# Four feature blocks per step for one-tile chunks in a fused attention and two-layer kernel

## The chip, the cores and the metric

The kernel runs on one core of a Trainium2 chip. The metric is the device time of one execution in microseconds. Three runs of the kernel before gave 1259.59, 1261.18 and 1263.39 us, median 1261.18.

## The reference

The inputs are q, k and v of shape (4 batches, 8 heads, 576 positions, 64), and five weights. Attention keeps, in each row of scores, the 32 largest and softmaxes over them. Its output, as 2304 tokens of 512 features, goes through two layers:

```python
scores = scale * np.matmul(q, k.transpose(0, 1, 3, 2))
kth = np.partition(scores, -32, axis=-1)[..., -32:-31]
scores = np.where(scores >= kth, scores, -1e9)
attn = softmax(scores)                  # rows of 576
x = np.matmul(attn, v)                  # -> 2304 x 512
gate = 1.0 / (1.0 + np.exp(-(x @ w_gate)))        # 512 -> 1536
x = (gate * (x @ w_val)) @ w_out                  # 1536 -> 512
g = np.maximum(x @ w_in, 0.0) ** 2                # 512 -> 2048
out = g @ w_out2                                  # 2048 -> 512, float32
```

## The kernel before

The 2304 tokens are 18 tiles of 128. They are worked in 12 chunks (line 29): chunks 0 to 5 hold one tile each, chunks 6 to 11 two. For every chunk, attention is done first (8 heads per tile: scores on TensorE, four rounds of the eight largest on VectorE, the exponential on ScalarE, the transposed weights times the values on TensorE), then the two layers.

N is the number of tokens in a chunk, 128 or 256. Chunks 0 and 1 use a function of their own in float32 (`moe32`, lines 902 to 996). Chunks 2 to 11 split every operand into a high and a low float16 part and use three products of these per block (`SPLIT`, line 694). A feature block is 128 features: the first layer has NF1 = 12 of them, the second NF2 = 16.

One step of layer 1 is `l1_pair` (lines 744 to 770). For two feature blocks it makes the gate matmuls into a bank `pg` and the value matmuls into a bank `pv` (12 matmuls of N columns for each block), then a chain: Tanh on ScalarE (line 763), an add-and-multiply on GpSimd (764), the product with `pv` on VectorE (765), the high part as a cast on ScalarE (768), the low part as a difference on GpSimd (769). `l1_acc` (lines 780 to 800) then multiplies the result by `w_out` into two accumulators. It is written one step behind `l1_pair`, so that a step's chain runs beside the next step's matmuls.

Between the layers the accumulators are squared and summed for a scale (lines 822 to 830) and split in two parts (832, 833). One step of layer 2 is `l2_pair` (851 to 872): matmuls into a bank `ph`, ReLU (867) and Square (869) on ScalarE, a square in float32 and a difference on GpSimd (870, 871); then `l2_acc` (874 to 885) with the output weights, written DEPTH2 = 3 steps behind. After the last step the output is copied (897) and stored.

The tiles `pg`, `pv` and `ph` share two PSUM banks (pool `ps_w`, 512 float32 columns each); the accumulators have two, attention four. The activation tiles `th`, `gh`, `r`, `rh` and the output tile share four buffers of the tag `hi` (HIB, line 27). From chunk 4 on (`PRE0`, line 41), a chunk calls `start` for the first two steps of the next chunk near its own end of layer 1 (lines 811, 836); their results have a buffer of their own, `gp`.

The order of the work on each engine is not written out. The kernel is written as a list of instructions with priorities, and a planner runs a simulated time at build and puts each engine's instructions in order by priority and by when they can start, giving out buffers as they come free. Each engine then takes its instructions strictly in that order. Attention is written into this list by `attend` (line 1162): after each step of a chunk's layers, as many units of attention (one head of one tile) are written, with a higher priority, as `step` asks (line 1253), so that a whole chunk's attention is spread evenly over the steps of the chunk before.

Of the kernel before, what the change touches and what calls it, by code (L numbers as in the profile page):

```python
# [8 lines left out]
F16 = mybir.dt.float16  # L9
BF16 = mybir.dt.bfloat16  # L10
F32 = mybir.dt.float32
# [3 lines left out]
AF = mybir.ActivationFunctionType  # L15
ALU = mybir.AluOpType
# [5 lines left out]
P = 128  # L22
# [3 lines left out]
M4 = 3  # L26
HIB = 4
DEPTH2 = 3
CHUNKS = [[0], [1], [2], [3], [4], [5]] + [[i, i + 1] for i in range(6, 18, 2)]
AHEAD = 1000  # L30
LEAD = 10
# [8 lines left out]
NPRE = 2  # L40
# [29 lines left out]
TB = 15  # L70
# [3 lines left out]
def tile_topk_attention__then__two_moe_layers(  # L74
# [11 lines left out]
    chunks=None,  # L86
    upto=None,
):
    nc = tc.nc
    B, H, S, D = q.shape  # L90
# [3 lines left out]
    KM = DM // P  # L94
    NF1 = F1 // P
    NF2 = F2 // P
# [8 lines left out]
    if chunks is None:  # L105
        chunks = CHUNKS

# [3 lines left out]
    mpool = ctx.enter_context(tc.tile_pool(name="mpool", bufs=1))  # L111
# [172 lines left out]
    class Pair:  # L284


        def __init__(self, ci, hp, xt):
            self.ci, self.hp, self.xt = ci, hp, xt
            self.tts = chunks[ci]
            self.N = len(self.tts) * P  # L290
            self.segs = segments(ci)
# [234 lines left out]
        def values(self):  # L526
            xp = ps_t.tile([P, 512], F32, tag="tr", name=f"xp_{self.ci}_{self.hp}")
            for si, (b, o, n) in enumerate(self.segs):
                for c in range(NB):
                    for j in range(2):  # L530
# [12 lines left out]
                        )  # L543
            nc.scalar.copy(self.xt[:, self.hp, :], xp[:, 0 : self.N])

# [143 lines left out]
    def wblk(name, a, kt, f0, n):  # L689
        t, e = parts[(name, kt, f0 // 512)]  # L690
        return t[:, a, e, f0 % 512 : f0 % 512 + n]

    xsl = {}
    SPLIT = ((0, 0), (0, 1), (1, 0))
# [26 lines left out]
    class Moe:  # L721
        pass

    ahead = {}

    def start(ci):

        m = ahead[ci]
        if m.gp is None:
            m.gp = mpool.tile([P, NPRE, 2, 2 * m.N], F16, tag="m4", bufs=M4, name=f"gp_{ci}")  # L730
        fp = len(m.queue)
        m.queue.append((fp, m.l1_pair(fp, m.gp[:, fp])))

    def moe_head(ci, x):
        m = ahead[ci] = Moe()
        m.gp, m.queue = None, []
        tts = chunks[ci]
        N = len(tts) * P
        ig = scales["wg"][1]
        xs, ix = x  # L740
        gsc = xsmall[ci].bitcast(F32)[:, 4:5]
        nc.vector.scalar_tensor_tensor(gsc, ix, 0.5, ig, op0=ALU.mult, op1=ALU.mult)

        def l1_pair(fp, gh=None):
            pg = ps_w.tile([P, 512], F32, tag="wk", name=f"pg_{ci}_{fp}")
            pv = ps_w.tile([P, 512], F32, tag="wk", name=f"pv_{ci}_{fp}")
            for pp, wd in ((pg, "wg"), (pv, "wv")):
                for e in range(2):
                    f0 = (2 * fp + e) * P
                    n = 0  # L750
                    for c in range(KM):
                        for a, b_ in SPLIT:
                            nc.tensor.matmul(  # L753
                                pp[:, e * N : (e + 1) * N],
                                wblk(wd, a, c, f0, P),
                                xs[:, b_, c, :],
                                start=(e == 0 and n == 0),
                                stop=(n == 3 * KM - 1),
                                skip_group_check=True,
                            )  # L760
                            n += 1
            th = mpool.tile([P, 2 * N], F32, tag="hi", bufs=HIB, name=f"th_{ci}_{fp}")
            nc.scalar.activation(th, pg[:, 0 : 2 * N], AF.Tanh, scale=gsc)  # L763
            nc.gpsimd.tensor_scalar(th, th, 1.0, float(2.0 ** (-TB - 1)), op0=ALU.add, op1=ALU.mult)
            nc.vector.tensor_tensor(th, pv[:, 0 : 2 * N], th, op=ALU.mult)  # L765
            if gh is None:
                gh = mpool.tile([P, 2, 2 * N], F16, tag="hi", bufs=HIB, name=f"gh_{ci}_{fp}")
            nc.scalar.copy(gh[:, 0], th)  # L768
            nc.gpsimd.tensor_tensor(gh[:, 1], th, gh[:, 0], op=ALU.subtract)
            return gh  # L770

        m.N, m.ix, m.l1_pair = N, ix, l1_pair

    def moe(ci, nxt=None):

        m = ahead.pop(ci)
        tts, N, ix, l1_pair = chunks[ci], m.N, m.ix, m.l1_pair
        accs = []

        def l1_acc(fp, gh):  # L780
            if not accs:
                for h in range(2):
                    accs.append(ps_a.tile([P, 512], F32, tag="acc", name=f"acc1_{ci}_{h}"))

            last = fp == NF1 // 2 - 1
            for e, d in sorted(
                ((e, d) for e in range(2) for d in range(KM)),
                key=lambda t: (t[1], t[0]) if last else t,
            ):
                f = 2 * fp + e  # L790
                if True:
                    for x, (a, b_) in enumerate(SPLIT):
                        nc.tensor.matmul(  # L793
                            accs[d // 2][:, (d % 2) * N : (d % 2 + 1) * N],
                            wblk("wo", a, f, d * P, P),
                            gh[:, b_, e * N : (e + 1) * N],
                            start=(f == 0 and x == 0 and d % 2 == 0),
                            stop=(f == NF1 - 1 and x == 2),
                            skip_group_check=True,
                        )  # L800

        queue = m.queue
        depth = max(1, len(queue))
        for fp in range(len(queue), NF1 // 2):
            queue.append((fp, l1_pair(fp)))
            yield
            if len(queue) > depth:
                l1_acc(*queue.pop(0))
# [41 lines left out]

        def l2_pair(fp):
            ph = ps_w.tile([P, 512], F32, tag="wk", name=f"ph_{ci}_{fp}")
            for e in range(2):
                f0 = (2 * fp + e) * P

                terms = [(c, a, 0) for c in range(KM) for a in range(2)] + [(c, 0, 1) for c in range(KM)]
                for n, (c, a, b_) in enumerate(terms):
                    nc.tensor.matmul(  # L858
                        ph[:, e * N : (e + 1) * N],
                        wblk("wi", a, c, f0, P),  # L860
                        x2[:, b_, c, :],
                        start=(e == 0 and n == 0),
                        stop=(n == 3 * KM - 1),
                        skip_group_check=True,
                    )
            r = mpool.tile([P, 2 * N], F32, tag="hi", bufs=HIB, name=f"r_{ci}_{fp}")
            nc.scalar.activation(r, ph[:, 0 : 2 * N], AF.Relu, scale=float(2.0 ** (7 - 2 * TB)))
            gh = mpool.tile([P, 2, 2 * N], F16, tag="hi", bufs=HIB, name=f"rh_{ci}_{fp}")
            nc.scalar.activation(gh[:, 0], r, AF.Square)  # L869
            nc.gpsimd.tensor_tensor(r, r, r, op=ALU.mult)  # L870
            nc.gpsimd.tensor_tensor(gh[:, 1], r, gh[:, 0], op=ALU.subtract)  # L871
            return gh

        def l2_acc(fp, gh):
            for e in range(2):
                f = 2 * fp + e
                for i in range(len(tts)):
                    for x, (a, b_) in enumerate(SPLIT):
                        nc.tensor.matmul(  # L879
                            acc2[i][:, 0:DM],  # L880
                            gh[:, b_, e * N + i * P : e * N + (i + 1) * P],
                            wblk("w2", a, f, 0, DM),
                            start=(f == 0 and x == 0),
                            stop=(f == NF2 - 1 and x == 2),
                        )

        prev = []
        for fp in range(NF2 // 2):
            prev.append((fp, l2_pair(fp)))
            if len(prev) > DEPTH2:  # L890
                l2_acc(*prev.pop(0))
            yield
        for p in prev:
# [108 lines left out]
    nchunk = len(chunks)  # L1002
# [164 lines left out]
    first = [0]  # L1167
    for c in chunks:
        first.append(first[-1] + H * len(c))
    per_chunk = NF1 // 2 + NF2 // 2  # L1170

    base = 100000

    def at(t):
# [63 lines left out]
    for ci in range(len(PLAIN), nchunk):  # L1238
        while ci not in xsp and ci not in ahead:
            attend(emitted[0] + 1, AHEAD)  # L1240
        if ci not in ahead:
            moe_head(ci, xsp.pop(ci))
        nxt = None
        if PRE0 <= ci < nchunk - 1:

            def nxt(c=ci + 1):
                if c not in ahead:
                    while c not in xsp:
                        attend(emitted[0] + 1, AHEAD)
                    moe_head(c, xsp.pop(c))  # L1250
                start(c)

        step = H * len(chunks[min(ci + 1, nchunk - 1)]) / per_chunk
        lead = LEAD if ci < PRE0 else LEAD2
        for n, _ in enumerate(moe(ci, nxt)):
            attend(first[ci + 1] + lead + int((n + 1) * step), AHEAD)
# [33 lines left out]
```

## Time and profile before

| | |
|---|---|
| runs | 1259.59, 1261.18, 1263.39 us |
| span of the profiled execution | 1261.3 us (no time besides the span is shown for it) |
| TensorE busy | 1176.1 us, 93% |
| VectorE busy | 954.8 us, 76% |
| ScalarE busy | 828.6 us, 66% |
| GpSimd busy | 846.5 us, 67% |
| mean clock of TensorE, share of full | 0.978 |
| layers of chunks 2 to 5 | about 316 to 600 us |

The busy time of an engine is the time covered by its instructions; matmuls are pipelined and their ends are modelled. A wait is idle time of an engine ahead of an instruction, put down to the operation that released it last. In a matmul row, "128*128 128x256" means weights of 128 by 128 and 256 moving columns.

### The profile page before, as it was taken

To read this page: it belongs to the slowest core of one execution; us is meant where nothing else is said; L and a number is where in the kernel's file an instruction comes from. 1 tells how busy PE (TensorE), PEld (TensorE's weight loads), DVE (VectorE), ACT (ScalarE), POOL (GpSimd) and SP (SyncE) were. 2 spreads that over 40 slices of the span, in tenths; PEclk is the share of its full clock that TensorE was granted. 3 is DMA by queue.
4 is the path that set the end of the run, shared out by engine and by line. 5 is a ranking of instruction groups with operands and counts; after the bars stand their busy time and mean duration, and the time that the engine had idled before them with its cause. 6 is when DMAs were issued, how large, how long until landed. Compare 5 with 4: busy or idle time off the path is not lost.

```text
span 1261.3 us, 30690 instructions
## 1 busy us (share of the span) xinstructions
PE 1176.1 (93%) x11477; PEld 957.5 (76%) x11477; DVE 954.8 (76%) x1965; ACT 828.6 (66%) x1719; POOL 846.5 (67%) x1294
## 2 busy tenths in 40 slices
PE   6757989999889998899998999999999999999998
PEld 5536877987777877779787778877876887787775
DVE  6998789899977978899988899999789969110010
ACT  4998996577767676677776777776567657322122
POOL 1788774488876577797876987797678659425223
PEclk9986999999989999999999999999999999999999
DMA  7988762223344356665776575567434523200000
GB/s 188 366 298 275 260 199 81 59 76 90 113 131 130 81 125 159 143 136 130 137 157 133 125 181 115 127 140 158 77 73 97 116 54 60 53 2 1 17 1 18
DMA packets 243190, 153.94 MB, mean 122 GB/s; under 512 B 193120, under 2 KB 209504, under 8 KB 243040
## 3 DMA queue, kind: packets, MB, share of 16 engines
q1 hardware_dynamic: 243040, 151.97, 47.7%
q8 instruction: 91, 1.49, 0.5%
q14 instruction: 59, 0.48, 0.1%
HBM read 105.51 MB, written 18.09 MB: 98 GB/s over the span
## 4 chain that ended last, share of the span: by engine, by line
PE 67%; ACT 9%; POOL 7%; DVE 7%; DMA 5%; issue 3%; SPq 2%; POOLq 0%; ACTq 0%; DVEq 0%
PE ph L858 12%; PE acc L879 12%; PE acc L793 8%; PE pg L753 8%; PE pv L753 8%; PE sp L376 5%; PE xp L509 3%; DMA PT<-S 3%; DVE mx L392 2%; PE xp L536 2%; DVE W L399 2%; PE pg L912 1%; PE qpt L336 1%; PE ph L959 1%; PE acc L976 1%
## 5 line engine op out<-in xcount | busy, mean ns | idle before, releaser
L392 DVE MAX8 mx<-W 128x8 f32<-128x576 f32 x432 | 327.9, 759 | 11.2
L399 DVE MATCH_REPLACE8 W<-mx,W 128x576 f32<-128x576 f32 x288 | 213.8, 742 | 0.0
L858 PE MATMUL ph<-x,wi_w 128*128 128x256 f16 (+1 forms) x1920 | 190.9, 253 | 2.7 <-ACT x L832 2.6
L879 PE MATMUL acc<-w_w,rh 128*128 128x512 f16 x768 | 182.2, 379 | 0.9 <-POOL rh L871 0.9
L858 PEld LDWEIGHTS <-wi_w 128*128 128x128 f16 x1920 | 156.4, 99 | 29.0 <-issue 4.0
L753 PE MATMUL pg<-xs,wg_w 128*128 128x256 f16 (+1 forms) x1440 | 148.4, 254 | 1.1 <-ACT th L763 0.8
L753 PE MATMUL pv<-xs,wv_w 128*128 128x256 f16 (+1 forms) x1440 | 143.8, 252 | 5.1 <-DVE th L765 3.7
L376 PE MATMUL sp<-kst,qt 128*128 128x288 f32 x608 | 132.9, 330 | 6.5 <-ACT rh L869 2.5
L457 POOL TENSOR_TENSOR S<-W,S 128x512 f16<-128x512 f32 x192 | 137.0, 735 | 2.1
L379 ACT COPY S<-sp 128x576 f32<-128x576 f32 x144 | 91.8, 638 | 66.3 <-PE sp L376 39.7
L793 PEld LDWEIGHTS <-wo_w 128*128 128x128 f16 x1440 | 119.6, 99 | 19.2 <-issue 7.4
L411 ACT ACTIVATE W<-S,mx 128x576 f32<-128x576 f32 x144 | 111.8, 776 | 30.9 <-DVE mx L392 30.5
L753 PEld LDWEIGHTS <-wg_w 128*128 128x128 f16 x1440 | 118.9, 99 | 17.2 <-issue 1.4
L753 PEld LDWEIGHTS <-wv_w 128*128 128x128 f16 x1440 | 117.4, 98 | 18.1 <-issue 5.8
L765 DVE TENSOR_TENSOR th<-pv,th 128x512 f32<-128x512 f32 (+1 forms) x60 | 34.7, 579 | 125.4 <-PE pv L753 121.0
L879 PEld LDWEIGHTS <-rh 128*128 128x128 f16 x768 | 72.0, 98 | 73.3 <-POOL rh L871 1.2
L392 DVE MAX8 mx<-S 128x8 f32<-128x576 f32 x144 | 107.3, 745 | 25.9 <-ACT S L379 24.1
L793 PE MATMUL acc<-gh,wo_w 128*128 128x256 f16 (+1 forms) x1104 | 105.6, 250 | 4.7 <-ACT gh L768 2.6
L399 DVE MATCH_REPLACE8 W<-mx,S 128x576 f32<-128x576 f32 x144 | 106.9, 742 | 0.0
L455 POOL TENSOR_SCALAR W<-W,bs 128x576 f32<-128x576 f32 x96 | 71.6, 746 | 52.6 <-ACT S L454 47.8
L870 POOL TENSOR_TENSOR r<-r 128x512 f32<-128x512 f32 (+1 forms) x80 | 69.6, 869 | 54.8 <-ACT rh L869 54.1
L376 PEld LDWEIGHTS sp<-kst,qt 128*128 128x128 f32 x608 | 90.8, 192 | 17.5 <-issue 3.8
(246 smaller groups left out, 2331.5 us busy)
## 6 DMA issues: line engine op xcount, KB each, us to landing
kst<-ks SPq DMA_DIRECT2D x112, 288.0 KB, 3.1
v<-vd SPq DMA_DIRECT2D x32, 320.0 KB, 3.3
qn<-in_q_dram SPq DMA_DIRECT2D x128, 64.0 KB, 2.3
wi_r<-in_moe_w_in_dram SPq DMA_DIRECT2D x16, 512.0 KB, 6.2
w_r<-in_moe_w_out_dram SPq DMA_DIRECT2D x16, 512.0 KB, 4.5
v<-in_v_dram SPq DMA_DIRECT2D x56, 128.0 KB, 2.4
wg_r<-in_moe_w_gate_dram SPq DMA_DIRECT2D x12, 512.0 KB, 6.0
wv_r<-in_moe_w_val_dram SPq DMA_DIRECT2D x12, 512.0 KB, 7.3
```

The costliest lines, as they stand in the source:

```text
L376: nc.tensor.matmul(sp[:, e, 0:HALF], l, r, start=(x == 0), stop=(x == len(ops) - 1))
L379: nc.scalar.copy(ss.rearrange("p (e s) -> p e s", e=2), sp[:, :, 0:HALF])
L392: m8 = nc.vector.max(mx[:, min(r, 1)], cur)
L399: nc.vector.match_replace(wk, mx[:, min(r, 1)], cur, NEG)
L411: nc.scalar.activation(wk, ss, AF.Prelu, bias=kth, scale=-1.0, alpha=1.0 / BIG)
L455: nc.gpsimd.tensor_scalar(wk, wk, rz, 1.0, op0=ALU.mult, op1=ALU.mult)
L457: nc.gpsimd.tensor_tensor(pp[:, o : o + e - f], wk[:, f:e], pp[:, f:e], op=ALU.subtract)
L753: nc.tensor.matmul(pp[:, e * N : (e + 1) * N], wblk(wd, a, c, f0, P), xs[:, b_, c, :], start=(e == 0 and n == 0), stop=(n == 3 * KM - 1), ...
L793: nc.tensor.matmul(accs[d // 2][:, (d % 2) * N : (d % 2 + 1) * N], wblk("wo", a, f, d * P, P), gh[:, b_, e * N : (e + 1) * N], start=(f == ...
L858: nc.tensor.matmul(ph[:, e * N : (e + 1) * N], wblk("wi", a, c, f0, P), x2[:, b_, c, :], start=(e == 0 and n == 0), stop=(n == 3 * KM - 1) ...
L870: nc.gpsimd.tensor_tensor(r, r, r, op=ALU.mult)
L879: nc.tensor.matmul(acc2[i][:, 0:DM], gh[:, b_, e * N + i * P : e * N + (i + 1) * P], wblk("w2", a, f, 0, DM), start=(f == 0 and x == 0), s ...
```

## The change

A chunk of N tokens takes W = 512 / N feature blocks per step: four for chunks 2 to 5, two, as before, for chunks 6 to 11. A step's tiles `pg`, `pv`, `ph`, `th`, `gh`, `r`, `rh` are then 512 columns wide for every chunk. Layer 1 of a one-tile chunk has 3 steps in place of 6, layer 2 has 4 in place of 8. In layer 2 the accumulation of a one-tile chunk is written DEPTH1 = 2 steps behind. `start` makes two steps ahead, so eight feature blocks in place of four when the next chunk is chunk 5. The units of attention are spread over 7 steps in place of 14.

```diff
+DEPTH1 = 2
...
+    def per_step(N):
+
+        return 512 // N
+
...
-            m.gp = mpool.tile([P, NPRE, 2, 2 * m.N], F16, tag="m4", bufs=M4, name=f"gp_{ci}")
+            m.gp = mpool.tile([P, NPRE, 2, m.W * m.N], F16, tag="m4", bufs=M4, name=f"gp_{ci}")
...
         N = len(tts) * P
+        W = per_step(N)
...
-                for e in range(2):
-                    f0 = (2 * fp + e) * P
+                for e in range(W):
+                    f0 = (W * fp + e) * P
...
-            th = mpool.tile([P, 2 * N], F32, tag="hi", bufs=HIB, name=f"th_{ci}_{fp}")
-            nc.scalar.activation(th, pg[:, 0 : 2 * N], AF.Tanh, scale=gsc)
+            th = mpool.tile([P, W * N], F32, tag="hi", bufs=HIB, name=f"th_{ci}_{fp}")
+            nc.scalar.activation(th, pg[:, 0 : W * N], AF.Tanh, scale=gsc)
...
-            last = fp == NF1 // 2 - 1
+            last = fp == NF1 // W - 1
             for e, d in sorted(
-                ((e, d) for e in range(2) for d in range(KM)),
+                ((e, d) for e in range(W) for d in range(KM)),
                 key=lambda t: (t[1], t[0]) if last else t,
             ):
...
-        for fp in range(len(queue), NF1 // 2):
+        for fp in range(len(queue), NF1 // W):
...
-            for e in range(2):
-                f0 = (2 * fp + e) * P
+            for e in range(W):
+                f0 = (W * fp + e) * P
...
-            r = mpool.tile([P, 2 * N], F32, tag="hi", bufs=HIB, name=f"r_{ci}_{fp}")
+            r = mpool.tile([P, W * N], F32, tag="hi", bufs=HIB, name=f"r_{ci}_{fp}")
...
-        for fp in range(NF2 // 2):
+        for fp in range(NF2 // W):
             prev.append((fp, l2_pair(fp)))
-            if len(prev) > DEPTH2:
+            if len(prev) > (DEPTH2 if W == 2 else DEPTH1):
                 l2_acc(*prev.pop(0))
...
-        step = H * len(chunks[min(ci + 1, nchunk - 1)]) / per_chunk
+        W = per_step(len(chunks[ci]) * P)
+        step = H * len(chunks[min(ci + 1, nchunk - 1)]) / (NF1 // W + NF2 // W)
```

## Rows read from the trace of the kernel before

**Rows 1.** Stretches: length, busy us of PE, PEld, DVE, ACT, POOL, clock, DMA.

```profile
...
316.00:600.00 284.00, 259.60 (x3496) 224.81 (x3494) 244.34 (x547) 202.21 (x480) 207.89 (x376) 0.97 0.52 128
600.00:1100.00 500.00, 495.06 (x4826) 391.15 (x4825) 427.05 (x886) 338.68 (x710) 378.92 (x622) 1.00 0.54 113
...
```

**Rows 2.** TensorE's waits, 316 to 600 us: waiter, releaser, us, times, longest.

```profile
...
PE kpt L164 <- DMA kn<-in_k_dram: 5.5, 3, 2.8
PE pv L753 <- DVE th L765: 3.7, 1, 3.7
PE acc L793 <- ACT gh L768: 2.6, 1, 2.6
PE sp L376 <- ACT rh L869: 2.5, 1, 2.5
PE acc L793 <- POOL gh L769: 2.0, 2, 1.6
PE acc L793 <- ACT ob L897: 1.9, 1, 1.9
...
PE acc L879 <- POOL rh L871: 0.9, 2, 0.6
PE pg L753 <- ACT th L763: 0.8, 1, 0.8
...
```

**Rows 3.** Timeline, chunk 2's layer 1: start, us, engine, line, operation, [idle before].

```profile
...
333.90 1.50 PE L793 MATMUL acc<-gh,wo_w 128*128 128x128 f16 x24
...
337.17 2.23 DVE L666 SCALAR_TENSOR_TENSOR w_w<-w_c,wsmall,w_w 128x1024 f16<-128x1024 f32 x1
...
339.99 0.40 DVE L765 TENSOR_TENSOR th<-pv,th 128x256 f32<-128x256 f32 x1
...
340.45 2.06 PE L753 MATMUL pv<-xs,wv_w 128*128 128x128 f16 x24 [3.70 <-DVE th L765]
...
342.58 2.46 PE L753 MATMUL pg<-xs,wg_w 128*128 128x128 f16 x24
...
```

**Rows 4.** Timeline of TensorE, end of layer 1 and layer 2 of chunk 2.

```profile
...
357.64 1.50 PE L793 MATMUL acc<-gh,wo_w 128*128 128x128 f16 x24
361.76 0.37 PE L793 MATMUL acc<-gh,wo_w 128*128 128x128 f16 x2 [2.61 <-ACT gh L768]
363.68 2.29 PE L793 MATMUL acc<-gh,wo_w 128*128 128x128 f16 x20 [1.55 <-POOL gh L769]
...
378.68 1.46 PE L879 MATMUL acc<-w_w,rh 128*128 128x512 f16 x6
...
```

**Rows 5.** Timeline, start of layer 2 of chunk 4.

```profile
...
524.49 2.85 PE L858 MATMUL ph<-x,wi_w 128*128 128x128 f16 x48
...
527.76 0.64 ACT L379 COPY S<-sp 128x576 f32<-128x576 f32 x1 [2.37 <-DMA PT<-S]
...
529.84 0.77 PE L376 MATMUL sp<-kst,qt 128*128 128x288 f32 x4 [2.50 <-ACT rh L869]
...
```

**Rows 6.** Instructions on two tiles: count, duration ns min/median/max, first, last, forms.

```profile
...
L764 POOL TENSOR_SCALAR th<-th x60: 395/617/626, 322.0 to 1201.7; 128x512 f32<-128x512 f32 x36, 128x256 f32<-128x256 f32 x24
L765 DVE TENSOR_TENSOR th<-pv,th x60: 400/678/693, 323.5 to 1203.6; 128x512 f32<-128x512 f32 x36, 128x256 f32<-128x256 f32 x24
L768 ACT CAST gh<-th x46: 387/601/622, 324.1 to 1204.3; 128x512 f16<-128x512 f32 x24, 128x256 f16<-128x256 f32 x22
L769 POOL TENSOR_TENSOR gh<-th,gh x46: 662/1152/1168, 324.7 to 1205.0; 128x512 f16<-128x512 f32 x24, 128x256 f16<-128x256 f32 x22
...
L867 ACT ACTIVATE r<-ph x80: 359/597/617, 374.8 to 1247.7; 128x512 f32<-128x512 f32 x48, 128x256 f32<-128x256 f32 x32
L869 ACT ACTIVATE rh<-r x80: 400/618/654, 375.2 to 1249.8; 128x512 f16<-128x512 f32 x48, 128x256 f16<-128x256 f32 x32
L870 POOL TENSOR_TENSOR r<-r x80: 606/1038/1047, 375.7 to 1250.6; 128x512 f32<-128x512 f32 x48, 128x256 f32<-128x256 f32 x32
L871 POOL TENSOR_TENSOR rh<-r,rh x80: 666/1153/1172, 376.4 to 1251.7; 128x512 f16<-128x512 f32 x48, 128x256 f16<-128x256 f32 x32
...
```

More of the change, by code (lines that the diff above doesn't have):

```diff
@@ L761, in l1_pair @@
                             n += 1
-            th = mpool.tile([P, 2 * N], F32, tag="hi", bufs=HIB, name=f"th_{ci}_{fp}")
-            nc.scalar.activation(th, pg[:, 0 : 2 * N], AF.Tanh, scale=gsc)
+            th = mpool.tile([P, W * N], F32, tag="hi", bufs=HIB, name=f"th_{ci}_{fp}")
+            nc.scalar.activation(th, pg[:, 0 : W * N], AF.Tanh, scale=gsc)
             nc.gpsimd.tensor_scalar(th, th, 1.0, float(2.0 ** (-TB - 1)), op0=ALU.add, op1=ALU.mult)
-            nc.vector.tensor_tensor(th, pv[:, 0 : 2 * N], th, op=ALU.mult)
+            nc.vector.tensor_tensor(th, pv[:, 0 : W * N], th, op=ALU.mult)
             if gh is None:
-                gh = mpool.tile([P, 2, 2 * N], F16, tag="hi", bufs=HIB, name=f"gh_{ci}_{fp}")
+                gh = mpool.tile([P, 2, W * N], F16, tag="hi", bufs=HIB, name=f"gh_{ci}_{fp}")
             nc.scalar.copy(gh[:, 0], th)
@@ L770, in l1_pair @@
             return gh
-        m.N, m.ix, m.l1_pair = N, ix, l1_pair
+        m.N, m.W, m.ix, m.l1_pair = N, W, ix, l1_pair
     def moe(ci, nxt=None):
         m = ahead.pop(ci)
-        tts, N, ix, l1_pair = chunks[ci], m.N, m.ix, m.l1_pair
+        tts, N, W, ix, l1_pair = chunks[ci], m.N, m.W, m.ix, m.l1_pair
         accs = []
@@ L783, in l1_acc @@
                     accs.append(ps_a.tile([P, 512], F32, tag="acc", name=f"acc1_{ci}_{h}"))
-            last = fp == NF1 // 2 - 1
+            last = fp == NF1 // W - 1
             for e, d in sorted(
-                ((e, d) for e in range(2) for d in range(KM)),
+                ((e, d) for e in range(W) for d in range(KM)),
                 key=lambda t: (t[1], t[0]) if last else t,
             ):
[L790 to L800, printed above, removed]
+                f = W * fp + e
+                for x, (a, b_) in enumerate(SPLIT):
+                    nc.tensor.matmul(
+                        accs[d // 2][:, (d % 2) * N : (d % 2 + 1) * N],
+                        wblk("wo", a, f, d * P, P),
+                        gh[:, b_, e * N : (e + 1) * N],
+                        start=(f == 0 and x == 0 and d % 2 == 0),
+                        stop=(f == NF1 - 1 and x == 2),
+                        skip_group_check=True,
+                    )
         queue = m.queue
         depth = max(1, len(queue))
-        for fp in range(len(queue), NF1 // 2):
+        for fp in range(len(queue), NF1 // W):
             queue.append((fp, l1_pair(fp)))
@@ L865, in l2_pair @@
                     )
-            r = mpool.tile([P, 2 * N], F32, tag="hi", bufs=HIB, name=f"r_{ci}_{fp}")
-            nc.scalar.activation(r, ph[:, 0 : 2 * N], AF.Relu, scale=float(2.0 ** (7 - 2 * TB)))
-            gh = mpool.tile([P, 2, 2 * N], F16, tag="hi", bufs=HIB, name=f"rh_{ci}_{fp}")
+            r = mpool.tile([P, W * N], F32, tag="hi", bufs=HIB, name=f"r_{ci}_{fp}")
+            nc.scalar.activation(r, ph[:, 0 : W * N], AF.Relu, scale=float(2.0 ** (7 - 2 * TB)))
+            gh = mpool.tile([P, 2, W * N], F16, tag="hi", bufs=HIB, name=f"rh_{ci}_{fp}")
             nc.scalar.activation(gh[:, 0], r, AF.Square)
@@ L874, in l2_acc @@
         def l2_acc(fp, gh):
-            for e in range(2):
-                f = 2 * fp + e
+            for e in range(W):
+                f = W * fp + e
                 for i in range(len(tts)):
@@ L1169, in tile_topk_attention__then__two_moe_layers @@
         first.append(first[-1] + H * len(c))
-    per_chunk = NF1 // 2 + NF2 // 2
     base = 100000
```

## The prediction

> **What bounds the kernel now.** I read the busy time of each engine by stage first. The chunks the change touches, 2 to 5 (one tile of 128 tokens each), run their two layers from 316 to about 600 us. There TensorE works 259.6 of 284 us, so 24.4 us are idle, at a mean clock of 0.97; VectorE works 244.3 (86%), ScalarE 202.2 (71%) and GpSimd 207.9 (73%) [rows 1]. From 600 to 1100 us TensorE is busy 495 of 500 us with VectorE at 427 [rows 1]: no chunk there is touched, and as TensorE has nothing to spare and VectorE 73 us, what TensorE gains before 600 us should arrive at the end, and so should what it loses. So the first thing to look at is TensorE's idle time in this stage.
>
> The list of TensorE's waits gives that time names [rows 2]. Six entries belong to the steps of the two layers: the value matmuls on VectorE's product (3.7), the down matmuls on ScalarE's cast (2.6) and GpSimd's difference (2.0), a score matmul behind the squares of layer 2 (2.5), a down matmul behind the output copy (1.9), and two small ones (0.9 and 0.8). That is 14.4 us. Another 5.5 us wait for key loads, which the change does not touch. A stall also lowers the clock: after the 3.70 us wait, 24 matmuls take 2.46 us where the same 24 took 1.50 before it [rows 3]; the clock of 0.97 over 284 us is about 8.5 us lost in the stage.
>
> **What the change removes.** The matmuls are the same in number and shape; only their grouping differs. In layer 1 three steps replace six, in layer 2 four replace eight, in each of four chunks: 12 and 16 steps fewer. Two operations of 256 columns become one of 512. The shortest of each operation's durations is its 256-column form, the median its 512-column form [rows 6]. In microseconds, GpSimd's add-and-multiply goes from 2 x 0.395 to 0.617, VectorE's product from 2 x 0.400 to 0.678, ScalarE's cast from 2 x 0.387 to 0.601, GpSimd's difference from 2 x 0.662 to 1.152; in layer 2 ReLU from 2 x 0.359 to 0.597, Square from 2 x 0.400 to 0.618, GpSimd's square from 2 x 0.606 to 1.038, its difference from 2 x 0.666 to 1.153. So GpSimd saves 12 x 0.34 + 16 x 0.35 = 9.7 us, ScalarE without Tanh 12 x 0.17 + 16 x 0.30 = 6.9 us, VectorE 12 x 0.12 = 1.5 us. I cost these savings at nothing by themselves: TensorE is the busier engine in this stage, and all three have idle time. Their worth is in queue delays, which stand in the next part.
>
> **What it moves.** Each step now holds four feature blocks, so while one step's chain of ScalarE, GpSimd and VectorE runs, TensorE has twice the matmuls of the neighbouring steps to do. Twenty-four matmuls of 128 columns show 1.50 us [rows 3] and overlap their successor, so I count 1.4. Against it, the chain of each step is longer. After the last value matmul of layer 1 it grows by 0.28 (product) + 0.21 (cast) + 0.49 (difference) = 0.98 us, in layer 2 by 0.24 + 0.22 + 0.43 + 0.49 = 1.38 us [rows 6]. The queue delays inside the chain do not grow with the width, and in the long waits they are most of it. Place by place:
>
> Middle of layer 1, chunk 2. The value matmuls waited 3.70 us for VectorE's product, which stood behind a weight split of 2.23 us among others [rows 3]. Between one step's value matmuls and the next lie a down group and a gate group; both double, so the cover grows by 2.8 us, the need by 0.22 + 0.28 = 0.5. The wait falls by 2.3, and the lower clock behind it costs perhaps 0.6 less: -2.9. Bounds: none of it, if the split is only met elsewhere, and 3.7 + 1.7 with the clock.
>
> End of layer 1, chunk 2. A down group of 24 matmuls is the only cover, and 2.61 and 1.55 us are idle behind it [rows 4]. Cover grows by 1.4, need by 0.98: -0.4. Bounds -4.2 and +1.0. The other three ends show no such wait; there the longer chain has cover from attention, or from the next chunk's first steps, which for chunk 5 become twice as large.
>
> Start of layer 2, chunk 4. Two working banks of ph are filled in 2.85 us, then TensorE idles 2.50 us at a score matmul while ScalarE stands on a transpose's transfer (2.37 us) and then copies and squares in order [rows 5]. Two banks now hold 2.8 us more work, the chain's ReLU and Square need 0.46 more. If the score matmul only waited for its turn, 2.3 us go; if its own transfer was late, nothing. I take -1.5, nearer to the cover.
>
> The output copy (1.9), with 2.8 us more work in front but on an engine in strict order: -1.0 (bounds -1.9, 0). The two small ones (1.7): -1.0, because hand-overs are half as many (bounds -1.7, 0).
>
> Costs. Layer 2 keeps two wide steps in flight where it kept three narrow ones. Six of its down matmuls show 1.46 us [rows 4], so the last step's chain is covered by 24 matmuls in place of 18, about 1.4 us more, against 1.38 more need: even. The four shared activation buffers are filled exactly (one square in work and three finished steps), which can hold up a ReLU where the difference of the step before is late. The planner also orders every engine's queue anew, and a new order has stalls of its own. No row shows these. Below, they cost nothing; above, all eight ends (two layers, four chunks) pay the chain's growth in full, 4 x (0.98 + 1.38) = 9.4 us. I take +2.0, nearer to nothing because the cover grows as much as the need.
>
> **The sum.** -2.9 - 0.4 - 1.5 - 1.0 - 1.0 + 2.0 = -4.8 us. The profiled span is 1261.3 us and the median of the three runs 1261.18, so the profile stands for the runs and almost nothing lies around it. 1261.3 - 4.8 = 1256.5 us.
>
> **Rivals.** (A) The forecast, 1256.5: hand-overs are half as many, each with twice the cover. For it: the named waits stand behind other work in queues, which does not widen.
>
> (B) The waits belong to attention and the new order only moves them. For it: the product stood behind a weight split, and ScalarE behind a transpose's transfer [rows 3, 5]; neither is touched. Against it: TensorE got to those points with its own cover used up. Time: 1261.3, give or take 3.
>
> (C) The longer chain decides: slower. The wider product, cast and difference give their first column of use later, and at the ends of the layers TensorE has nothing else to do. Price: 0.98 and 1.38 us per end, 9.4 us if all eight pay and no wait is shortened, 1270.7; with half of the gains kept, about 1267. It decides where the covering group is not placed behind the last chain; in chunk 2 the chain's 4.2 us idle show such a place [rows 4]. Against it: the cover grows with the chain. The Trainium skill (Perfetto Trace Analysis, Optimizing Scalar/DVE Operations) says that grouping into larger operations helps a saturated engine, and that where ScalarE and VectorE are not saturated but cause bubbles elsewhere, breaking up instructions may let work complete sooner. The shares of 71% and 86% are the second case, so by that rule the change goes the wrong way and (C) holds; no row here shows a wider step beside a narrow one of the same chunk.
>
> (D) All six kinds of wait vanish, 14.4 us, with their share of the clock, 8.5 x 14.4 / 24.4 = 5.0: 1242. For it: GpSimd and ScalarE lose 16.6 us of work, and attention's own chain gets shorter. Against it: half of these waits have a reason outside the layers.
>
> **How the numbers follow.** A 0.42, D 0.10, B 0.24, C 0.24. A difference under 0.3% (3.8 us) can't be told from none here. The forecast lies just beyond that, so a sliver of A is inside it and of B outside, which cancel: faster 0.52, same 0.24, slower 0.24. The range leaves out the last part of D and the worst of C: 1246 to 1269.
>
> **What would show it.** In the changed profile the gate, value and ph matmuls of chunks 2 to 5 stand in groups of 48, and 128x256 forms of the nine step operations remain only in chunks 0 and 1, which another function computes. TensorE's idle time between 316 us and the end of chunk 5 should be near 20 us in place of 24.4, the wait on VectorE's product 1.5 us or less, the clock 0.97 or above, and 600 to 1100 us unchanged. GpSimd's total should fall by about 10 us and ScalarE's by 7 to 10. The forecast is wrong if the idle time at the ends of layers grows by a microsecond or more each (C), if key loads or transposes' transfers take up the freed time (B), or if a gain before 600 us does not arrive at the end because VectorE then sets the pace.

## The result: 0.66% slower, outside the forecast

| | before | changed |
|---|---|---|
| median | 1261.89 us (4 runs, 1259.59 to 1263.39) | 1270.15 us (4 runs, 1268.35 to 1272.29) |
| ratio, 95% interval | | 1.0066 [1.005, 1.0083] |
| profiled execution: span, own time | 1261.3 us, not shown | 1268.9, 1270.66 us |
| TensorE, VectorE, ScalarE, GpSimd busy | 1176.1, 954.8, 828.6, 846.5 us | 1175.9, 953.4, 822.4, 836.8 us |

The forecast was 1256.5 us in a range of 1246 to 1269: the sign is wrong, and the time lies 1 us beyond the range. The stages of the changed kernel answer to [rows 1]; the two short stretches lie inside them (same columns).

```profile
316.00:600.00 284.00, 258.62 (x3515) 223.97 (x3514) 234.74 (x515) 191.26 (x418) 194.07 (x318) 0.96 0.53 124
560.00:600.00 40.00, 31.70 (x399) 28.23 (x397) 37.79 (x83) 24.99 (x53) 25.42 (x46) 0.87 0.68 142
640.00:700.00 60.00, 51.81 (x507) 43.35 (x506) 54.01 (x120) 39.92 (x91) 38.26 (x67) 0.89 0.61 142
600.00:1100.00 500.00, 489.90 (x4723) 384.56 (x4722) 436.23 (x906) 342.49 (x715) 380.87 (x623) 0.99 0.53 116
```

The same two short stretches of the kernel before:

```profile
560.00:600.00 40.00, 37.80 (x525) 33.92 (x523) 37.03 (x85) 28.66 (x64) 28.98 (x53) 1.00 0.58 132
640.00:700.00 60.00, 55.73 (x576) 47.90 (x574) 51.74 (x114) 41.86 (x92) 43.14 (x72) 1.00 0.68 141
```

In these 100 us TensorE is idle 16.5 us in place of 6.5, and at a clock of 0.87 and 0.89 in place of full speed, while VectorE is as busy as before or more. The waits of TensorE from 316 to 600 us answer to [rows 2]:

```profile
PE xp L510 <- DMA PT<-S: 8.6, 3, 6.9
PE kpt L165 <- DMA kn<-in_k_dram: 4.4, 3, 2.6
PE ph L863 <- ACT x L837: 3.2, 1, 3.2
PE ph L863 <- ACT r L872: 2.5, 1, 2.5
PE x2pq L830 <- ACT x L828: 2.4, 1, 2.4
```

All waits that the forecast named are gone from this list (it speaks of six entries; its 14.4 us are seven). Three at hand-overs of the layers have grown (ph behind x from 0.2, x2pq behind x from 0.5, ph behind ReLU is new), and one is attention's: 6.9 us for the transposed weights of a head. In TensorE's timeline, the first four lines answer to [rows 3 and 4], the fifth to [rows 5], and the last three are that wait:

```profile
338.53 2.84 PE L759 MATMUL pg<-xs,wg_w 128*128 128x128 f16 x48
341.21 2.34 PE L759 MATMUL pv<-xs,wv_w 128*128 128x128 f16 x39
...
353.41 0.73 PE L798 MATMUL acc<-gh,wo_w 128*128 128x128 f16 x10
354.89 2.18 PE L798 MATMUL acc<-gh,wo_w 128*128 128x128 f16 x36
...
520.88 4.42 PE L863 MATMUL ph<-x,wi_w 128*128 128x128 f16 x76
...
571.44 0.22 PE L510 MATMUL xp<-PT,v 128*64 128x128 f16 x1
578.55 1.65 PE L510 MATMUL xp<-PT,v 128*64 128x128 f16 x27 [6.89 <-DMA PT<-S]
...
581.71 3.04 PE L759 MATMUL pg<-xs,wg_w 128*128 128x256 f16 x14
```

Gate and value matmuls stand in groups of up to 48 with no wait between them, the down matmuls at the end of layer 1 wait for neither the cast nor the difference, and the ph matmuls run on. Of chunk 6's layers TensorE can do only nine gate and nine value matmuls (at 563 to 565 us) before the last heads of its attention are handed over as input (xs). That comes at 580.23 us, and behind the idle 7 us 14 gate matmuls take 3.04 us. In the kernel before it came at 567.92, and the layers took it up at 582.16 (changed, then before):

```profile
580.23 0.28 ACT L524 ACTIVATE xs<-xp 128x128 f16<-128x128 f32 x1 [0.62 <-PE xp L510]
...
567.92 0.28 ACT L523 ACTIVATE xs<-xp 128x128 f16<-128x128 f32 x1 [0.49 <-PE xp L509]
...
582.16 2.78 PE L753 MATMUL pg<-xs,wg_w 128*128 128x256 f16 x24
```

So attention had 14.2 us of slack there; now it is 12.3 us later and TensorE stands ready for it from 571.7 us. Operations on [rows 6] keep their 512-column durations, as here:

```profile
L872 ACT ACTIVATE r<-ph x64: 573/597/627, 376.5 to 1255.3; 128x512 f32<-128x512 f32 x64
```

So the layers were quicker and attention came later. Two marks show it. The scale at the end of layer 1 (line 847, before 842) is done, in chunks 2 to 5, 7.2, 3.6, 3.7 and 5.6 us earlier than before, in chunk 6 6.4 us later and from chunk 7 on 9 to 10 us later. And the start of each head's top-32 on VectorE (the first MAX8, on a tile S; 144 "units", counted from 0) is level with before at unit 36, 1.3 to 7.5 us late from 39 to 51, and 12.3 us late at unit 53. Chunk 6 holds units 48 to 63. Where the 12 us arise, VectorE's timeline shows, with the last of the four value scales (vsc) from which the factor of chunk 6's softmaxes (ix) is made, the units' first maxima, the scale of chunk 5's input (x_5s), the factor itself, the load that begins a unit's replacement, and the mark in chunk 5. Changed kernel:

```profile
384.48 0.14 DVE L136 TENSOR_SCALAR vsc<-vs 128x1 int32<-128x1 int32 x1
...
450.68 0.74 DVE L393 MAX8 mx<-S 128x8 f32<-128x576 f32 x1
456.36 0.74 DVE L393 MAX8 mx<-S 128x8 f32<-128x576 f32 x1
457.94 0.28 DVE L706 TENSOR_REDUCE x_5s<-x_5pq 128x1 f32<-128x128 f32 x1
458.14 0.15 DVE L266 TENSOR_REDUCE ix<-vsc 128x1 f32<-128x4 f32 x1
462.80 0.74 DVE L393 MAX8 mx<-S 128x8 f32<-128x576 f32 x1
469.75 0.09 DVE L400 MATCH_VALUE_LOAD W<-mx,S 128x8 f32 x1 [6.14 <-POOL S L458]
...
489.84 0.76 DVE L393 MAX8 mx<-S 128x8 f32<-128x576 f32 x1 [3.61 <-ACT S L380]
...
590.05 0.21 DVE L847 SCALAR_TENSOR_TENSOR x2s<-x_5s,x2s,wsmall 128x1 f32<-128x1 f32 x1
```

Kernel before:

```profile
385.96 0.14 DVE L135 TENSOR_SCALAR vsc<-vs 128x1 int32<-128x1 int32 x1
...
449.10 0.76 DVE L392 MAX8 mx<-S 128x8 f32<-128x576 f32 x1 [2.86 <-ACT S L379]
451.62 0.15 DVE L265 TENSOR_REDUCE ix<-vsc 128x1 f32<-128x4 f32 x1
455.06 0.74 DVE L392 MAX8 mx<-S 128x8 f32<-128x576 f32 x1
460.95 0.74 DVE L392 MAX8 mx<-S 128x8 f32<-128x576 f32 x1
462.07 0.09 DVE L399 MATCH_VALUE_LOAD W<-mx,S 128x8 f32 x1 [0.38 <-POOL S L457]
...
477.50 0.74 DVE L392 MAX8 mx<-S 128x8 f32<-128x576 f32 x1
...
595.60 0.20 DVE L842 SCALAR_TENSOR_TENSOR x2s<-x_5s,x2s,wsmall 128x1 f32<-128x1 f32 x1
```

Before, two units of chunk 6 stand ahead of the factor, 48 (at 438.59) and 49. In the changed kernel three do, 48 (444.96), 49 and 50, and the factor comes 6.5 us later. No unit of the chunk can end without the factor, so each keeps its buffer W and its S. There are three W: unit 51 finds none. What hangs on that is seen on GpSimd (POOL), the load queue (SPq) and TensorE of the changed kernel:

```profile
461.45 0.63 POOL L419 TENSOR_SCALAR bs<-bs,xfc 128x1 f32<-128x1 f32 x2
468.29 2.80 POOL L458 TENSOR_TENSOR S<-W,S 128x512 f16<-128x512 f32 x4
469.74 3.25 SPq L460 DMA_TRANSPOSE PT<-S  x2
474.86 1.27 SPq L152 DMA_DIRECT2D kn<-in_k_dram  x2
478.63 1.08 PE L165 MATMUL kpt<-ident,kn 128*128 128x128 f32 x4 [2.58 <-DMA kn<-in_k_dram]
```

Two units are ended together; only then a W is free (VectorE's 6.14 us), then an S, into which the next keys are loaded (474.86; before 465.45), and with them the scores of unit 53. It starts at 489.84 in place of 477.50.

### The profile page after: what moved, and what is told of

Same layout as the page of the kernel before. It is cut to its first block, busy times and chain, and to the rows that moved or that the text cites. A ratio compares the mean times of both kernels' runs of the same rounds, so it can differ in the third digit from the quotient of the medians.

```text
span 1268.9 us, 30514 instructions
## 1 busy us (share of the span) xinstructions
PE 1175.9 (93%) x11477; PEld 956.0 (75%) x11477; DVE 953.4 (75%) x1953; ACT 822.4 (65%) x1663; POOL 836.8 (66%) x1238
## 4 chain that ended last, share of the span: by engine, by line
PE 52%; DVE 17%; POOL 9%; ACT 9%; DMA 6%; issue 4%; SPq 2%; POOLq 0%; DVEq 0%; ACTq 0%
PE ph L863 9%; PE acc L884 9%; DVE mx L393 7%; PE pv L759 7%; PE pg L759 6%; DVE W L400 6%; PE acc L798 6%; PE sp L377 4%; DMA PT<-S 3%; PE xp L510 2%; POOL S L458 2%; PE pg L917 1%; PE xp L537 1%; PE ph L964 1%; PE acc L981 1%
## 5 line engine op out<-in xcount | busy, mean ns | idle before, releaser
L863 PE MATMUL ph<-x,wi_w 128*128 128x256 f16 (+1 forms) x1920 | 188.1, 252 | 7.2 <-ACT x L837 4.8
L884 PE MATMUL acc<-w_w,rh 128*128 128x512 f16 x768 | 179.1, 379 | 0.0
L377 PE MATMUL sp<-kst,qt 128*128 128x288 f32 x608 | 133.8, 332 | 11.9 <-ACT S L380 5.6
L393 DVE MAX8 mx<-S 128x8 f32<-128x576 f32 x144 | 107.4, 746 | 25.4 <-ACT S L380 25.4
L798 PEld LDWEIGHTS <-wo_w 128*128 128x128 f16 x1440 | 116.2, 98 | 11.3
L771 DVE TENSOR_TENSOR th<-pv,th 128x512 f32<-128x512 f32 x48 | 32.8, 684 | 116.4 <-PE pv L759 116.1
L455 ACT ACTIVATE S<-W,bs 128x576 f16<-128x576 f32 x96 | 74.2, 773 | 45.0 <-DVE bs L451 44.8
L875 POOL TENSOR_TENSOR r<-r 128x512 f32<-128x512 f32 x64 | 66.5, 1039 | 49.7 <-ACT rh L874 48.1
```

The source lines that it names most:

```text
L377: nc.tensor.matmul(sp[:, e, 0:HALF], l, r, start=(x == 0), stop=(x == len(ops) - 1))
L393: m8 = nc.vector.max(mx[:, min(r, 1)], cur)
L455: nc.scalar.activation(pp[:, 0:S], wk, AF.Copy, scale=rz)
L798: nc.tensor.matmul(accs[d // 2][:, (d % 2) * N : (d % 2 + 1) * N], wblk("wo", a, f, d * P, P), gh[:, b_, e * N : (e + 1) * N], start=(f == ...
L863: nc.tensor.matmul(ph[:, e * N : (e + 1) * N], wblk("wi", a, c, f0, P), x2[:, b_, c, :], start=(e == 0 and n == 0), stop=(n == 3 * KM - 1) ...
L884: nc.tensor.matmul(acc2[i][:, 0:DM], gh[:, b_, e * N + i * P : e * N + (i + 1) * P], wblk("w2", a, f, 0, DM), start=(f == 0 and x == 0), s ...
```

## The experiments

"Unit 55" is how late the 56th unit starts against before (489.56 us), "wait for W" the wait of VectorE near 468 us, "idle" what TensorE stands still in 560 to 600 and 640 to 700 us together, from one profile each. Each ratio is to the kernel before, run on the same chip; the runs were on several chips, on which the kernel before takes 1260.59 to 1263.04 us, so ratios compare better than medians.

| | edit | median us | ratio, 95% interval | unit 55 | wait for W | idle |
|---|---|---|---|---|---|---|
| before | | 1261.89 | | | 0.4 | 6.5 |
| changed | | 1270.15 | 1.0066 [1.005, 1.0083] | +12.0 | 6.1 | 16.5 |
| e1 | wide in layer 1 only | 1268.09 | 1.0033 [1.002, 1.0045] | +8.4 | 7.4 | 15.2 |
| e2 | wide in layer 2 only | 1272.92 | 1.0073 [1.0054, 1.0091] | +9.6 | 4.6 | 10.2 |
| e3 | wide groups, narrow operations | 1271.86 | 1.0070 [1.005, 1.009] | +8.4 | 5.9 | 8.7 |
| e4 | attention at 14 points | 1271.58 | 1.0061 [1.0043, 1.0078] | +9.1 | 7.2 | 15.7 |
| e5 | chunk 3 narrow | 1269.80 | 1.0073 [1.0051, 1.0094] | +8.4 | 5.4 | 9.9 |
| e6 | only chunk 3 wide | 1271.66 | 1.0086 [1.0067, 1.0106] | +5.7 | 6.4 | 8.8 |
| e7 | changed, two units more lead | 1264.83 | 1.0023 [1.0011, 1.0034] | +8.0 | 6.8 | 11.1 |
| e8 | before, attention at 7 points | 1266.18 | 1.0034 [1.0022, 1.0045] | -0.9 | 0.4 | 8.6 |
| s1 | changed, shorter attention | 1255.47 | 0.9948 [0.9928, 0.9968] | -8.3 | 5.2 | 2.2 |
| s2 | before, shorter attention | 1257.10 | 0.9964 [0.995, 0.9979] | -10.9 | 4.7 | 4.1 |
| c1 | before, two units more lead | 1267.87 | 1.0047 [1.0027, 1.0066] | 0.0 | 0.8 | 4.9 |
| c2 | changed, four units more | 1283.14 | 1.0166 [1.0151, 1.0181] | +15.2 | 3.4 | 5.0 |
| d1 | changed, one unit more | 1273.26 | 1.0091 [1.0065, 1.0117] | +10.6 | 6.1 | 16.5 |
| d2 | before, one unit more | 1265.78 | 1.0026 [1.0016, 1.0035] | -2.1 | 0.4 | 7.1 |
| d3 | changed, LEAD 12 alone | 1268.04 | 1.0041 [1.0027, 1.0054] | +8.2 | 6.8 | 9.2 |
| d4 | changed, LEAD2 16 alone | 1274.63 | 1.0088 [1.0061, 1.0114] | +9.1 | 6.2 | 15.6 |
| f1 | changed, own buffers for ix | 1256.98 | 0.9967 [0.9954, 0.9981] | +0.1 | none | 5.7 |
| f2 | before, own buffers for ix | 1272.37 | 1.0087 [1.0067, 1.0108] | -2.5 | none | 2.7 |

**Which part of the change (e1, e2, e5, e6).** The width is set for each layer and chunk by itself (diff of e1; e5 and e6 use `if ci != 3` and `if ci == 3`):

```diff
+    def per_step2(N):
+
+        return 2
...
-            for e in range(W):
+            for e in range(W2):
```

> Four blocks per step in layer 1 alone, layer 2 as before. Theory S (attention's pace on VectorE sets the time up to 600 us, and the wide steps delay its units by 12 us): each layer brings a part, 1263 to 1268 us, and unit 53 of attention starts between 484 and 490 us. Rival P (TensorE's own waits at the ends of the layers): layer 1 grows the chain by 0.98 us at four ends, 1262 to 1265 us with unit 53 near 484 us. Rival N (any new order of the queues moves the time by some 8 us, whatever the widths): anywhere from 1254 to 1270 us.

> Four blocks per step in layer 2 alone, layer 1 as before. Theory S: the rest of the loss, so that this and the run with layer 1 alone add up to about 8 us; in the changed kernel VectorE waited 6.1 us behind GpSimd's wide layer-2 squares and differences at 464 to 470 us, so this one should have the larger part, 1265 to 1270 us. Rival P: 1.38 us at four ends, 1264 to 1267 us. Rival N: no sum of parts, 1254 to 1270 us.

> Wide steps for chunks 2, 4 and 5, narrow for chunk 3. In the changed kernel attention falls behind in two places, 2 to 7 us while chunk 2 is in its layers and another 10 us at units 52 and 53, while chunk 3 is in layer 2. If the wide steps of chunk 3 do the harm there (theory M: wide groups of a layer whose inputs are ready fill TensorE's queue ahead of attention's small operations), this run keeps unit 53 before 484 us and takes 1258 to 1264 us. If the order as such (theory N), unit 53 may come anywhere, and the time lies between 1256 and 1272 us.

> Wide steps for chunk 3 alone. Theory M: most of the harm, unit 53 near 488 us, 1266 to 1271 us. Theory N: no relation to the run with all chunks but chunk 3 wide; 1256 to 1272 us.

Each layer alone makes it slower, together they cost no more than layer 2 alone, and one wide chunk (e6) costs as much as all four. That does not add up by steps or by ends of layers, so rival C's price per end is not what decides; nor do e1 and e2 add up to some 8 us, as S has it. M, which blames chunk 3's steps, falls with e5, which narrows them and stays as slow.

**The operations' width and the spread of attention (e3, e4, e8).** e3 keeps the groups of 48 matmuls and cuts each operation of the chain into halves of 256 columns; e4 gives attention its 14 places per chunk back; e8 gives the narrow kernel the 7 places of the changed one.

```diff
+            hs = [slice(o, o + 256) for o in range(0, W * N, 256)] if N == P else [slice(0, W * N)]
+            for h in hs:
+                nc.vector.tensor_tensor(th[:, h], pv[:, h], th[:, h], op=ALU.mult)
...
+            if W2 == 4:
+                yield
...
+            if len(chunks[ci]) == 1 and n % 2 == 0:
+                continue
```

> The changed kernel with each ScalarE, GpSimd and VectorE operation of the wide steps cut into two of 256 columns; the matmuls stay in groups of 48. If the width of these operations in strictly ordered queues is what delays attention (part of theory S), the loss of 8 us mostly goes: 1261 to 1264 us. If the groups on TensorE, the points at which attention is written in, or the order as such are the cause, it stays at 1268 to 1272 us.

> The changed kernel with attention written in at 14 points per one-tile chunk again, twice per wide step, and not at 7. If the coarser spread of attention over the steps is the cause (the other part of theory S), the loss goes: 1260 to 1264 us, unit 53 near 484 us. If not, 1268 to 1272 us and unit 53 near 490 us.

> The kernel before, narrow steps, with attention written in after every second step of the one-tile chunks, so at 7 points. Theory N (a change of order that touches no width): between 1256 and 1272 us, and not 1263; unit 53 near 486 us as in all four kernels so far whose order differs from the kernel before. Theories M and S with the width as cause: 1261 to 1265 us.

Neither gives the time back, so neither the longer operations nor the coarser spread is by itself the cause. e8, all narrow, is slower by 0.34% with its units in time until unit 91 (within 3 us) and 5 to 6 us late from 92 to 119, so a new order alone can cost half of what the change costs.

**Does attention's lateness carry the loss (e7, s1, s2)?** e7 writes attention in two units earlier; s1 and s2 shorten it in both kernels by leaving out the third of the four rounds of maximum and replacement in chunks 5 and 6.

```diff
-LEAD = 10
+LEAD = 12
-LEAD2 = 14
+LEAD2 = 16
...
             for r in range(TOPK // 8):
+                if r == 2 and 5 <= self.ci <= 6:
+                    marks.append(m8.ins)
+                    continue
```

> The changed kernel with attention written in two units earlier throughout (LEAD 12 and LEAD2 16 for 10 and 14). Theory S (attention late by 12 us leaves TensorE without work twice, at 572 to 578 us and near 670 us): if the distance in the list decides how far attention is ahead, the holes shrink by up to 8 us each and the time falls to 1256 to 1264 us. If attention is held by its own chain or by buffers, nothing changes: 1268 to 1272 us.

> Leaves out the third of four rounds of maximum and replacement in the 24 attention units of chunks 5 and 6 of the changed kernel (1.6 us of VectorE each, some 38 us in all), so that attention is early at units 48 to 63 whatever the layers do. Theory S (TensorE starves at 560-580 and 660-700 us because attention's units run some 12 us late): both holes close (TensorE busy 37 us or more of 560-600 and 55 or more of 640-700) and the time falls by 8 us or more, to 1262 or less. Theory P (longer chains in the layers cost): the chains are untouched, 1266-1271. Theory N (any new order of the queues moves the time by some us either way): within 8 us of 1270, and its gap to the same cut made in the kernel before stays 5 us or more in one of the two directions.

> The same cut (third round of maximum and replacement left out in chunks 5 and 6) in the kernel before. S: attention was in time there, so only its small holes (2.2 us in 560-600, 4.3 in 640-700) can close: 1255-1262, and the gap between this and the changed kernel with the cut shrinks from 8 us to 3 or less. P: gap unchanged, 6-9 us. N: 1254-1270 with no relation to the holes.

Against the changed kernel s1 falls by 14.7 us, against the kernel before s2 by 5.1 (1262.21 to 1257.10), and the gap of 8 us is gone: 1255.47 against 1257.10, with overlapping intervals. The chains in the layers were not touched, so P falls and S stands, and N's gap of 5 us or more did not appear. e7 gained 5 us and ended 0.8 us above S's range. s1's stretches (columns as above):

```profile
560.00:600.00 40.00, 39.98 (x567) 36.10 (x566) 38.32 (x84) 27.74 (x59) 28.66 (x49) 1.00 0.71 155
640.00:700.00 60.00, 57.85 (x567) 48.40 (x565) 51.35 (x112) 41.99 (x92) 41.79 (x69) 1.00 0.66 147
```

Both holes are closed, at full clock. The wait for W is still there in s1 (5.2 us), and s2 has one too; with units 8 to 11 us early it opens no hole.

**Is it the width or only the order (c1, c2, d1 to d4)?** LEAD and LEAD2 say how many units attention is ahead of its even spread, in chunks up to 3 and from chunk 4 on. They are changed as in e7, to 12 and 16 (c1), 14 and 18 (c2), 11 and 15 (d1, d2), 12 and 14 (d3), 10 and 16 (d4).

> The kernel before with attention written in two units earlier (LEAD 12 and 16 in place of 10 and 14). S: attention in time already, so 1258-1263. N: a new order of the same work, 1254-1270.

> The changed kernel with attention written in four units earlier (LEAD 14 and 18). S: at least as good as two units earlier (1264.8), 1259-1265, with units 53 on less than 8 us late. N: anywhere from 1260 to 1275, with no relation to the two-unit lead.

> The changed kernel with attention written in one unit earlier (LEAD 11 and 15). Theory S (attention's lateness is the cost, any order that brings it in time gets the time back): units 53 to 63 between 12 late (as changed) and 8 (two units of lead): 1264-1268, and the time follows the units' lateness at 560 to 700 us. Theory W (the wide steps cost about 0.6% by themselves, in whatever order): 1267-1272. Theory N (the order of the queues is a draw around a mean, and the kernel before holds a good one): anywhere in 1258-1275.

> The kernel before with attention written in one unit earlier (LEAD 11 and 15), narrow steps. N: most new orders of the narrow kernel are slower too, by 2 to 7 us like the two tried (e8 4.3, two units of lead 5.9): 1264-1270. W: narrow steps keep their time, 1259-1264. S: 1259-1270, faster than 1264 only if its units at 560 to 700 us are in time.

> The changed kernel with the longer lead for chunks up to 3 alone (LEAD 12, LEAD2 14). S: the lateness arises at units 39 to 53, which are written by chunks 3 and 4, so part of the gain of two units of lead in both (5.4 us) is here: 1264-1268. W: 1267-1272. N: anywhere in 1258-1275.

> The changed kernel with the longer lead from chunk 4 on alone (LEAD 10, LEAD2 16). S: units up to 48 as late as in the changed kernel, units 53 on earlier: 1264-1268. W: 1267-1272. N: anywhere in 1258-1275. A version under 1259 would beat both kernels.

More lead is no cure: of the changed kernel's five other leads two are better (e7, d3), three worse (c2, d1, d4). S missed c1, c2, d1 and d4, and theory W, which has the wide steps cost 0.6% in any order, missed d1, d2 and d4. The narrow kernel's new orders are slower as well, by 0.26 to 0.47%, as N expects: the kernel before holds a good order. But the two families differ in one thing. All twelve wide orders with whole attention show the wait for W (3.4 us or more) and unit 55 5.7 to 15.2 us late; the four narrow ones show neither (0.8 us at most, -2.1 to 0.0). The layers' marks agree: from chunk 5's to chunk 6's, eleven of the twelve lose 4.8 to 13.1 us against before (the changed kernel 11.9), the other three narrow ones 0.6 at most, s1 nothing; c2 does not fit, as it is 34 us late at chunk 2 already. Behind chunk 6 both families lose more, 2.6 to 10.8 us, so neither "unit 55" nor "idle" ranks the times: c2, the slowest, has the smallest idle time of the wide ones. That led to the last pair.

**What makes attention late (f1, f2).** The factor `ix` took one of three buffers that it shares with the scales of the layers' inputs, and came right behind x_5s in both kernels, though its data were there 73.7 us sooner (65.7 before; rows vsc and ix above). The edit gives it two of its own:

```diff
-            xts_ = xsmall[ci] = mpool.tile([P, 8], I32, tag="xsc", bufs=3, name=f"ix_{ci}")
+            xts_ = xsmall[ci] = mpool.tile([P, 8], I32, tag="ixs", bufs=2, name=f"ix_{ci}")
```

> The changed kernel with two buffers of their own (tag ixs) for the factor of a chunk's attention (tile ix, line 266). In every order with wide steps that was run, VectorE waits 4.6 to 7.4 us at about 468 us for a buffer W that GpSimd frees late, because the softmaxes of chunk 6 wait for this factor; in every order with narrow steps it does not. The factor's input (vsc) is ready at 446.6 us, but the factor is computed at 458.1, right behind the scale of chunk 5's input (x_5s), with which it shares three buffers. Theory F (that chain makes attention late): the wait goes, units 53 to 63 come 6 us or more earlier, the hole at 578 us closes, and the time falls to 1260-1265. Rival N (any new order): 1264-1275, wait or no wait. Rival L (attention loses its time elsewhere as well): the wait goes, but units 55 to 63 stay 8 us or more late, 1267-1271.

> The same two buffers in the kernel before. F: the factor was at 451.6 there and no such wait followed, so little to gain: 1258-1264; the gap to the changed kernel with the same edit is 3 us or less. N: 1262-1270. If f1 or this is under 1259, it beats both kernels.

(These texts give 4.6 us as the shortest wait of a wide order; it is 3.4, in c2. They also have the factor's data ready at 446.6 us. That row belongs to the values of the next batch: in f1 the factor is done at 383 us, right behind the row at 383.05 and ahead of the one at 445.14. The row in its place is the one at 384.48.) f1 is faster than both kernels: 0.9967 [0.9954, 0.9981] of before, and lower than F expected. Its VectorE timeline:

```profile
383.05 0.14 DVE L136 TENSOR_SCALAR vsc<-vs 128x1 int32<-128x1 int32 x1
383.23 0.16 DVE L266 TENSOR_REDUCE ix<-vsc 128x1 f32<-128x4 f32 x1
...
462.28 0.09 DVE L400 MATCH_VALUE_LOAD W<-mx,S 128x8 f32 x1
471.45 0.76 DVE L393 MAX8 mx<-S 128x8 f32<-128x576 f32 x1 [0.18 <-ACT S L380]
477.67 0.74 DVE L393 MAX8 mx<-S 128x8 f32<-128x576 f32 x1
...
576.08 0.20 DVE L847 SCALAR_TENSOR_TENSOR x2s<-x_5s,x2s,wsmall 128x1 f32<-128x1 f32 x1
```

and its stretches:

```profile
560.00:600.00 40.00, 39.96 (x533) 34.41 (x531) 37.94 (x83) 29.63 (x62) 30.11 (x49) 1.00 0.58 117
600.00:1100.00 500.00, 490.25 (x4673) 388.58 (x4672) 427.12 (x884) 334.18 (x689) 369.36 (x604) 0.99 0.51 113
```

The factor is done at 383 us, nothing waits for W, unit 53 starts at 477.67 (changed 489.84, before 477.50), the hole is gone, and the layers' mark in chunk 5 is 19.5 us earlier than before. Of that 6.8 us are left at chunk 10 (1123.81 against 1130.60): the units come 11 to 35 us late between 800 and 1000 us, and TensorE is idle 9.7 us of 600 to 1100 in place of 4.9. In the kernel before the same edit made it 0.87% slower, against F (1258 to 1264, and 3 us or less from f1, where it is 15.4) and beyond N (1262 to 1270). The units there are in time until unit 83 and 14 us late at 84; TensorE is busy 94.0 of 700 to 800 us.

The traces show why: the edit makes other factors late. With two buffers, the factor of a chunk comes only behind the layers' mark of two chunks before, which still reads that chunk's factor. In f2, chunk 6's mark and chunk 8's factor:

```profile
682.00 0.28 DVE L842 SCALAR_TENSOR_TENSOR x2s<-ix,x2s,wsmall 128x1 f32<-128x1 f32 x1
682.32 0.16 DVE L265 TENSOR_REDUCE ix<-vsc 128x1 f32<-128x4 f32 x1
```

With the three shared buffers of the kernel before this factor came at 597.23 us. The same stands at chunks 9 to 11 of f2 and at chunks 8 to 11 of f1, 0.3 to 1.1 us behind the mark each time. In both the lateness grows by 7 to 22 us at units 84, 100, 116 and 132, the fifth of each of these chunks: the unit ahead finds no W, as unit 51 did (f2: first maximum of unit 83 at 670.17, its load at 688.03). So f1 and f2 hold eight more cases of a late factor behind which attention falls back. Not tried are a third buffer of its own for the factor, and how much of f1's gain is the wide steps' and how much a good draw of the order.

## Why the prediction was wrong, step by step

**The step that failed** is the first: "what TensorE gains before 600 us should arrive at the end". It was argued from TensorE's 5 idle us of 500 against VectorE's 73 [rows 1]. That is a share of work, not what ends last. Attention runs one chunk ahead of the layers, and a chunk's layers wait for it. The 14.2 us by which it was ahead at chunk 6 were gone, 12.3 of them by its own lateness, and the layers' gain ran into that: 5.6 us ahead at chunk 5, 6.4 us behind at chunk 6. This turn of 12 us had no term in the sum. The text named "VectorE then sets the pace" as a way to be wrong; it was not VectorE's amount of work that did (it is busy 10 us less in 316 to 600 us than in [rows 1]) but a wait in its queue. s1 shows that the lateness carries the loss, and f1, with the eight late factors of f1 and f2, that a factor that comes late makes attention late. That f1 is also a new order, and that new orders alone move the narrow kernel by 0.3 to 0.5%, leaves open how the 0.66% divide.

**What the change removes** came as worked out: GpSimd -9.7 (9.7 forecast), ScalarE -6.2 (6.9), VectorE -1.4 us (1.5).

**The waits** went even further than the terms: all 14.4 us of them are gone, where the terms came to 6.8, 0.6 of it clock. The end of layer 1 in chunk 2 lost 4.2 us, its bound, not 0.4.

**The costs** were mis-sized: for +2.0, the three hand-overs grew by 2.5 + 3.0 + 1.9 = 7.4 us, inside the bound of 9.4. As a whole the layers' sum was near: -4.8 forecast, -14.4 + 7.4 = -7.0 in waits, 5.6 us earlier at chunk 5's mark.

**The rivals.** C gave the sign and the time (1267 to 1270.7), by the wrong mechanism, so that was luck: the price at ends of layers is paid, and the layers are early all the same. Its rule from the Trainium skill (Perfetto Trace Analysis, Optimizing Scalar/DVE Operations), that where ScalarE and VectorE are not saturated but cause bubbles elsewhere, breaking up instructions may let work complete sooner, finds no support here: e3 breaks the operations up and stays at 1.0070. B named the right waiter, transposes' transfers (0.5 to 8.6 us), but priced it at 3 us. D's waits vanished without D's time.

**The signs.** Idle time was 25.4 us, not 20; the clock 0.96, not 0.97; 600 to 1100 us lost 5.2 us of TensorE.

**What stays open:** what ties the wait for W to the wide steps. The count of units ahead of the factor is not it: e2 has two, as before, and waits 4.6 us. In e6 and e7 attention is level with before at unit 47 (0.4 us or less off) and the factor only 1 to 2 us later, but a W comes free 12.8 and 14.5 us behind the factor in place of 10.4; what GpSimd does in between was not taken apart.

## What to carry to other kernels

Before a gain on the busiest engine is carried to the end, look for the first place where another chain must hand it work, and how early that chain is there; a stage that runs ahead needs its own term in the sum. A small tile that shares a ring of buffers with an unrelated one inherits that one's lateness: ask of each producer that sits behind its data by many us which buffer it waits for, and give it enough of its own (two here made four later factors late). Where a planner orders the queues anew, time the neighbours of a kernel (one unit more lead, one point fewer) before a difference under 1% is put down to the edit.

## What the runs showed of the hardware

Behind the 6.89 us in which TensorE stood idle, 14 matmuls of 256 columns took 3.04 us (0.217 each), where matmuls of the same shape take 2.63 us for 24 (0.110) in its critical chain at 641 us. The granted clock is 0.50 from 579 to 581 us and 0.57 from 581 to 585, 1.00 from 641 to 645, so the slow matmuls stand at the lower level, 1.2 in place of 2.4 GHz.

```profile
641.55 2.63 PE pg L759 x24
```

So a hole costs more than its length: from 440 to 700 us the changed kernel's TensorE is busy only 3.3 us less than before (236.8 against 240.1), but at a mean clock of 0.95 against 0.99, at most 0.04 x 260 = 10 us by estimate (some of it falls into idle time, where it costs nothing). The two together are of the size of the 12 us that the layers lose there.
